# Local attention feeding a squared-ReLU MLP: attention output of tiles 6 and 7 transposed by DMA instead of on TensorE, with a new order of work

## The chip, the cores and the metric

The kernel runs on one core of a Trainium2 chip. The metric is the device time of one execution in microseconds (us); lower is better. The time before is 212.37 us, the median of five runs (211.97 to 212.8).

## The reference

Four batches, eight heads, 768 positions and head size 64. Each position sees eight global positions and the 96 positions up to itself, with a bias that grows with distance. The attention output, 3072 rows of 512, goes through two matrix products with a squared ReLU between them.

```python
scores = scale * np.matmul(q, k.transpose(0, 1, 3, 2))
is_global = pos[None, :] < int(n_global)               # n_global = 8
is_local = (rel >= 0) & (rel < int(n_local))           # n_local = 96
scores = scores + bias[None, :, :, :]
scores = np.where(is_global | is_local, scores, -1000000000.0)
a = np.exp(scores - np.max(scores, axis=-1, keepdims=True))
a = a / (np.sum(a, axis=-1, keepdims=True) + 1e-09)
x = np.matmul(a, v)              # then (B, S, H * D): 3072 x 512
h = x @ w_in                     # 512 -> 2048
g = np.maximum(h, 0.0) ** 2
return (g @ w_out).astype(np.float32)   # 2048 -> 512
```

## The kernel before

The 3072 rows are 24 tiles of 128 rows (index `j`, six per batch). Two tiles make a block of the MLP (index `blk`, 12 of them). A block's first product is done in eight steps `s1`, each 8 matmuls of 256 columns into one PSUM bank (L753); its second product is 16 steps `s2`, each 2 matmuls of 512 columns (L826).

For one tile the stages are:

- `load`: q, k and v are read by three DMAs on POOL's queue (L211). From tile 6 on, q and k go to a ring of three buffers, so that the load of tile j waits until the transposition of tile j-3 has read its buffer.
- `T`: q and k are transposed. Tiles 0 to 5 do it on TensorE (`tr`, L398) with a copy out of PSUM; from tile `JQK` = 6 on, one DMA transpose on SP's queue does it (L422). "T 12" below is this DMA for tile 12.
- `sc`: scores, 16 matmuls of 64 rows (8 for a batch's first tile) (L485). `exp` on ScalarE (L551), `mul` by the bias and mask on VectorE (L576).
- `pv`: probabilities times values, two halves of 8 matmuls (4 for a batch's first tile) (L638), and `norm` on VectorE, a reciprocal and a multiplication that write tile `x` (L665, L666).
- `xT`: `x` is transposed for the MLP. Tiles below `JX` do it with four TensorE transposes (`trx`, L701) and a copy out of PSUM by VectorE or ScalarE; tiles from `JX` on do it by one DMA transpose on SP's queue (L725). "xT 7" is this step for tile 7.

After `s1`, `relu` runs on ScalarE (L774) and the square `sq` on VectorE (L786). When a block's second product is complete, `o` copies it out of PSUM (L326 or L328) and `st` stores it by a DMA on SP's queue (L865); every block has two stores, "st 3" being those of block 3. At the end of the kernel the last block's second half is split in two.

So SP's queue carries the stores and all DMA transposes, in one order written at build time; what stands behind a DMA whose data is not ready waits with it.

The order of work on every engine is decided by `Plan.run` at build time, a list scheduler. Each operation has a cost, a set of predecessors and a `key`; the one with the earliest start (plus a small weight times its key) goes next. The tables `SHIFT` (by kind and tile), `LEADS` (by tile), `STEP` (after which `s1` step a tile's scores may come) and `HOLD` (which `s1` step waits for a tile's scores) move keys and predecessors. At run time the engines wait only for data and buffers; the order is fixed. Three one-element writes by VectorE (`gate`, L372) hold back the loads of tiles 8, 9 and 10; their predecessor in the plan is, among others, `xT_sp.get(j - 3)`, the DMA transposition of the output of tile j-3, where there is one.

The PSUM banks are a ring of six for everything but the sums of `s2`, which have two. `x` has two buffers: `norm` of tile j needs `x` of tile j-2 to have been transposed.

Of the kernel before, what the change touches and what calls it, by code (L numbers as in the profile page):

```python
# [21 lines left out]
class Plan:  # L22
# [8 lines left out]

    LAG = {"PE": 0.25, "ACT": 0.26, "DVE": 0.2, "SP": 0.6, "POOLQ": 0.8, "DMAQ": 1.2, "DMA": 0.0}
    URGE = 0.01
    SHIFT = {'T': -13, 'sc': -2.5, 'exp': -26, 'pv': -13, 'norm': -17, 'trx': -5, 'xT': 32, 'gk': -38, 'gv': -45, 'mul': -39, 'kl': 24, 's1': -3.5, 'relu': 8, 'sq': -13, 's2': -1.25, 'st': -30, ('mul', 4): 12, ('tr', 5): 18, ('T', 5): 8, ('norm', 5): -22, ('sc', 6): 16, ('pv', 6): 46, ('mul', 7): 29.5, ('gk', 7): -13, ('trx', 7): 12, ('sc', 8): -4, ('pv', 8): 9, ('norm', 9): -10, ('pv', 11): 14, ('pv', 12): 48, ('sc', 13): -14, ('pv', 14): 30, ('mul', 15): 17, ('norm', 17): 4, ('norm', 18): -36, ('exp', 19): -7, ('exp', 20): 14, ('pv', 20): 34, ('sc', 22): 10, ('s1', 2): -2.5, ('s1', 3): -32, ('sq', 3): 4, ('s1', 5): 9, ('s1', 6): 23.5, ('s1', 7): 34, ('s1', 8): -10, ('s2', 0): 7.5, ('s2', 2): -4, ('s2', 3): -27, ('s2', 4): 7.5, ('s2', 5): 22, ('s2', 6): 14, ('s2', 7): -4, ('s2', 8): -10, ('s2', 9): -8, ('s2', 10): -2}

    def shift(self, name):
        early = name[-1 if name[0] in ("T", "tr") else 1]
        return self.SHIFT.get(name[0], 0.0) + self.SHIFT.get((name[0], early), 0.0)

# [65 lines left out]
def kernel(  # L105
# [35 lines left out]
    NFIRST = 4  # L141
    NSPLIT = 4
    NBIAS = 3
    JQK, JX = 6, 8
    NQ, NKT = 3, 2 * TPB
    NG = 8 - NACC
    G = ("g", NG)
# [7 lines left out]
    def const(shape, dt, name):  # L155
        return consts.tile(shape, dt, name=name, tag=name)
# [18 lines left out]
    pbt = const([P, 2, P], FP32, "pbt")  # L175
    pbw = const([P, 2, P], FP32, "pbw")
    plan = Plan()
    LEADS = {5: 29.5, 6: 59, 7: 21, 8: 15, 9: 40, 10: 38, 11: 24, 12: 46, 13: 0, 14: 22, 15: 1, 16: -27, 17: 18, 18: -20, 19: 20, 20: 33, 22: 28, 23: 8}
    SAFE = {j: 1.6 for j in range(6, 12)} | {14: 4.2, 15: 3.2, 16: 3.5}
    SAFEX = {9: 1.5, 11: 1.5, 13: 2.5}  # L180

# [2 lines left out]
    JOIN = {(21, 0), (16, 0), (23, 0), (18, 0), (20, 0), (15, 0)}  # L184
    COPY = [14, 15, 19, 20, 22]
    BEHIND = {}
    HOLD = ((6, 0), (19, 0))
    STEP = {(17, 0): 58, (19, 0): 68, (4, 0): -7, (6, 0): 16, (11, 0): 24, (12, 0): 37}
    JGATE = 11
    NHS = 14  # L190
    NWARM = 8
# [68 lines left out]
    def emit_ones(e, js):  # L260
        for j in js:
            nc.vector.memset(v_sb[j][:, :, D : D + 1], 1.0)
# [38 lines left out]
    for g in range(NFIRST + 2, NT, 6):  # L301
        js = range(g, min(g + 6, NT))
        o = plan.op(
            ("ones", g), {"DVE": 0.2}, lambda e, js=js: emit_ones(e, js),
            key=-1.0, ready=15.0,
        )
# [40 lines left out]
    kl = [const([P, NPAIR, P], BF16, f"kl_{i}") for i in range(2 if COPY else 0)]  # L347
# [8 lines left out]
    for j in range(NT):  # L356
        b, t = divmod(j, TPB)
        first = t == 0
        need = 8 * (j // 2)
        base = need - LEADS.get(j, LEAD) + 4 * (j % 2)  # L360
        if (j, 0) in JOIN:
# [29 lines left out]
        for n in range(2) if j < JQK else ():  # L391
            users = []

            def emit_tr(e, j=j, n=n, fp=fp):
# [9 lines left out]
            tr = plan.op(  # L404
                ("tr", n, j), {"PE": 0.5 if fp else 0.24}, emit_tr,
                deps=[land["qk"[n], j]], key=base, takes=(*G, [users]),
            )
# [12 lines left out]
        if j >= JQK:  # L420
            def emit_dT(e, j=j, T_=T_):
# [5 lines left out]
            T = plan.op(  # L427
                ("T", j), {"SP": 1.3}, emit_dT,
                deps=[land["q", j], land["k", j], xT_op[j - 3]] + ku, key=base - 6,
            )  # L430
            T = plan.op(("moved", j), {"DMAQ": 1.2}, None, deps=[T])
            qk_users[slot(j)].append(T)
            if j in SAFE:

                T = plan.op(("seen", j), {"DMA": SAFE[j]}, None, deps=[T])
# [6 lines left out]
        mul, mul_users = {}, {}  # L442
# [55 lines left out]
        for gs in SETS.get(j, [tuple(range(groups))]):  # L498
            n = 8 * len(gs)
            sc_users = busers[2 * gs[0] : 2 * gs[-1] + 2]  # L500
            if (j, gs[0]) in JOIN:

                o, also, taken = joint
# [16 lines left out]
            if j < NBIAS:  # L520
# [6 lines left out]
            o = plan.op(  # L527
                ("sc", j, gs[0]), {"PE": 0.2 + 0.029 * n},
                lambda e, gs=also, f=emit_sc: f(e, gs), deps=[*deps, bias],
                key=base + 1 + 2 * gs[0], takes=takes,  # L530
            )
# [91 lines left out]
        norm = []  # L623
# [170 lines left out]
    for o in plan.ops:  # L794
        if o["name"][0] == "sc":
            j = o["name"][1]
            n = STEP.get(o["name"][1:], 4 * j - LEAD)
            if n >= 0 and j >= NFIRST:
                o["deps"].append(s1_ops[n // NSTEP, n % NSTEP])
                if o["name"][1:] in HOLD:  # L800
                    n += 1
                    s1_ops[n // NSTEP, n % NSTEP]["deps"].append(o)

    for blk in range(NBLK):
# [9 lines left out]
        for s, sub, half in order2:  # L814
# [5 lines left out]
            def emit_s2(e, blk=blk, s=s, sub=sub, half=half, w=w, cols=cols, own=own):  # L820
# [15 lines left out]
            o = plan.op(  # L836
                ("s2", blk, s, sub), {"PE": 0.43 * w / d_model}, emit_s2,
                deps=[d, land["wout", s]] + users[-1:],
                key=8 * blk + s + 2.0 + (0 if not last else 8 * sub + 8 * (half or 0)),
                takes=((*G, [users]) if own else ("acc", NACC, [users])) if s == 0 else None,  # L840
            )
# [6 lines left out]
            if s == NSTEP - 1:  # L848
# [14 lines left out]
                def emit_st(e, blk=blk, sub=sub, half=half, cols=cols):  # L863
# [7 lines left out]
                st = plan.op(  # L871
                    ("st", blk, sub), {"SP": 0.4}, emit_st,
                    deps=[ev, s1_ops[NLATE, 0] if blk < NLATE - 2 else None],
                    key=8 * blk + s + 9.0,
                )
                st = plan.op(("stored", blk, sub), {"DMAQ": 1.4}, None, deps=[st])
# [40 lines left out]
```

## Time and profile before

| | |
|---|---|
| Five runs | 211.97 to 212.8 us, median 212.37 |
| Profiled execution | 212.8 us, span from the first to the last instruction 211.0 |
| Granted TensorE clock | 1.00 |
| PE, VectorE, ScalarE, POOL busy | 204.0, 142.5, 119.4, 73.8 us |
| DMA queues, share of 16 engines' span | POOL's loads 88.0%, SP's stores and transposes 33.6% |

Times within the span are counted from its first instruction. A matmul's record is longer than the time until the next one can start, because matmuls overlap: the 768 matmuls of L753 have records of 273 ns each but follow each other every 109 ns or so (eight of them take 0.87 us in the chain of waits). Where a number of the prediction is a time on PE, it is taken from such stretches, not from the record of one matmul. About 24 of the 384 records of L826 are missing from this trace; the gaps that they leave are not waits.

### The profile page before, as it was taken

To read this page: it belongs to the slowest core of one execution; us is meant where nothing else is said; L and a number is where in the kernel's file an instruction comes from. 1 tells how busy PE (TensorE), PEld (TensorE's weight loads), DVE (VectorE), ACT (ScalarE), POOL (GpSimd) and SP (SyncE) were. 2 spreads that over 40 slices of the span, in tenths; PEclk is the share of its full clock that TensorE was granted. 3 is DMA by queue.
4 is the path that set the end of the run, shared out by engine and by line. 5 is a ranking of instruction groups with operands and counts; after the bars stand their busy time and mean duration, and the time that the engine had idled before them with its cause. 6 is when DMAs were issued, how large, how long until landed. Compare 5 with 4: busy or idle time off the path is not lost.

```text
span 211.0 us, 4998 instructions
## 1 busy us (share of the span) xinstructions
PE 204.0 (97%) x1960; PEld 142.9 (68%) x1984; DVE 142.5 (68%) x372; ACT 119.4 (57%) x222; POOL 73.8 (35%) x91
## 2 busy tenths in 40 slices
PE   7999999999999999999999999999999999999993
PEld 3777877666566856866856577686755766766862
DVE  7699688522887887883867684585785845953630
ACT  6787678134563754555753763754677436833531
POOL 8997675440638036422904040405400000000000
PEclk9999999999999999999999999999999999999999
DMA  9999999999799999999996979999933710310202
GB/s 131 146 174 187 183 191 199 175 161 235 77 173 130 211 114 126 201 169 137 149 175 71 198 83 96 144 131 134 141 105 75 169 33 3 124 26 3 99 0 99
DMA packets 112615, 27.32 MB, mean 129 GB/s; under 512 B 103248, under 2 KB 109648, under 8 KB 112592
## 3 DMA queue, kind: packets, MB, share of 16 engines
q0 software_dynamic: 79200, 13.37, 88.0%
q1 hardware_dynamic: 33392, 13.64, 33.6%
q8 instruction: 15, 0.25, 0.5%
q14 instruction: 8, 0.07, 0.1%
HBM read 27.26 MB, written 6.29 MB: 159 GB/s over the span
## 4 chain that ended last, share of the span: by engine, by line
PE 87%; DVE 7%; DMA 2%; issue 1%; ACT 1%
PE acc L826 38%; PE hT L753 36%; PE sc L485 5%; PE po L638 4%; DMA xT<-x 2%; DVE x L666 2%; PE warm L271 2%; PE tr L398 2%; DVE at L576 1%; DVE v L683 1%; DVE rs L665 1%; DVE qkT L328 1%; PE sc L465 1%; PE trx L701 1%; DVE hs L786 0%
## 5 line engine op out<-in xcount | busy, mean ns | idle before, releaser
L753 PE MATMUL hT<-xT,win 128*128 128x256 bf16 x768 | 94.2, 273 | 0.6 <-DMA xT<-x 0.4
L826 PE MATMUL acc<-wout,hs 128*128 128x512 bf16 (+1 forms) x376 | 90.1, 370 | 1.3 <-DVE rs L665 0.2
L774 ACT ACTIVATE hr<-hT 128x512 f32<-128x512 f32 x96 | 57.4, 605 | 54.7 <-PE hT L753 46.7
L753 PEld LDWEIGHTS <-win 128*128 128x128 bf16 x768 | 73.4, 98 | 17.9 <-issue 0.9
L786 DVE TENSOR_TENSOR hs<-hr 128x512 bf16<-128x512 f32 x96 | 65.3, 687 | 22.0 <-ACT hr L774 21.2
L826 PEld LDWEIGHTS <-hs 128*128 128x128 bf16 x400 | 36.9, 98 | 29.8
L551 ACT ACTIVATE esc<-sc 128x512 bf16<-128x512 f32 x78 | 40.4, 609 | 14.2 <-PE sc L485 13.4
L211 POOL DMA_DIRECT2D qk<-in_q_dram x23 | 20.6, 896 | 70.6 <-DMA qkT<-qk 52.7
L576 DVE TENSOR_TENSOR at<-esc,E 128x512 bf16<-128x512 bf16 x78 | 31.8, 421 | 8.7 <-ACT esc L551 6.3
L211 POOL DMA_DIRECT2D v<-in_v_dram x24 | 21.8, 910 | 1.4 <-DMA win<-in_moe_w_in_dram 1.0
L666 DVE TENSOR_TENSOR x<-po,rs 128x256 bf16<-128x256 f32 x48 | 20.4, 424 | 1.7
L211 POOL DMA_DIRECT2D qk<-in_k_dram x23 | 20.7, 906 | 0.5 <-DMA win<-in_moe_w_in_dram 0.5
L326 ACT COPY o<-acc 128x512 f32<-128x512 f32 (+1 forms) x20 | 11.2, 579 | 15.2 <-PE acc L826 15.1
L638 PEld LDWEIGHTS <-at 128*128 128x128 bf16 x352 | 15.8, 98 | 5.1 <-ACT at L551 0.5
L638 PE MATMUL po<-v,at 128*128 128x65 bf16 x352 | 17.6, 193 | 0.4 <-DVE v L683 0.2
L665 DVE RECIPROCAL rs<-po 128x4 f32<-128x4 f32 x48 | 8.5, 178 | 10.6 <-PE po L638 10.1
L485 PEld LDWEIGHTS <-qkT 64*128 64x128 bf16 x312 | 9.5, 94 | 6.1 <-issue 5.5
L485 PE MATMUL sc<-qkT 64*128 64x128 bf16 x192 | 12.9, 219 | 0.0
L485 PE MATMUL sc<-qkT,qkT 64*128 64x128 bf16 x120 | 8.6, 216 | 0.0
L328 DVE COPY o<-acc 128x512 f32<-128x512 f32 x5 | 3.5, 691 | 7.0 <-PE acc L826 7.0
L211 POOL DMA_DIRECT2D win<-in_moe_w_in_dram x8 | 6.2, 804 | 1.3 <-issue 0.5
L211 POOL DMA_DIRECT2D wout<-in_moe_w_out_dram x8 | 5.8, 720 | 2.1 <-DMA win<-in_moe_w_in_dram 2.0
(45 smaller groups left out, 69.1 us busy)
## 6 DMA issues: line engine op xcount, KB each, us to landing
out_dram<-o SPq DMA_DIRECT2D x23, 256.0 KB, 3.8
v<-in_v_dram POOLq DMA_DIRECT2D x24, 128.0 KB, 6.4
qk<-in_q_dram POOLq DMA_DIRECT2D x23, 128.0 KB, 4.7
qk<-in_k_dram POOLq DMA_DIRECT2D x23, 128.0 KB, 6.2
win<-in_moe_w_in_dram POOLq DMA_DIRECT2D x8, 256.0 KB, 8.0
wout<-in_moe_w_out_dram POOLq DMA_DIRECT2D x8, 256.0 KB, 9.1
qkT<-qk SPq DMA_TRANSPOSE x18, 5.5
plain<-in_q_dram SPq DMA_DIRECT2D x1, 256.0 KB, 3.3
```

The source lines that it names most:

```text
L211: nc.gpsimd.dma_start(out=dst, in_=src)
L326: nc.scalar.copy(dst, src)
L485: nc.tensor.matmul(out=tiles["sc", j, odd, g][:, at, :], lhsT=left[j - 1][half, pair, :] if kt else qkT[j % NKT][half, 1, pair, :], rhs=qk ...
L551: nc.scalar.activation(out=esc, in_=tiles.pop(("sc", j, odd, g)).rearrange("p a c -> p (a c)"), func=Act.Exp, scale=scale,)
L576: nc.vector.tensor_mul(at, tiles.pop(("esc", j, odd, g)), bias)
L638: nc.tensor.matmul(out=po[:, hi, :], lhsT=tiles["at", j, odd, g][:, at * P : (at + 1) * P], rhs=v_sb[kj][:, h, :], start=(i == 0), stop=(i ...
L665: nc.vector.reciprocal(rs, po[:, :, D : D + 1])
L666: nc.vector.tensor_tensor(out=x[:, 4 * hf : 4 * hf + 4, :], in0=po[:, :, :D], in1=rs.to_broadcast([P, 4, D]), op=Alu.mult,)
L753: nc.tensor.matmul(out=hT[:, c, :], lhsT=w_in_sb[s][:, kt, c * P : (c + 1) * P], rhs=tiles["xT", blk][:, kt, :], start=(kt == 0), stop=(kt ...
L774: nc.scalar.activation(hr, tiles.pop(("hT", blk, s)), Act.Relu)
L786: nc.vector.tensor_mul(hs, hr, hr)
L826: nc.tensor.matmul(out=tiles["acc", blk, sub, half], lhsT=hs[:, c, sub * P : (sub + 1) * P], rhs=w_out_sb[s][:, c, cols], start=(s == 0 an ...
```

## The change

`JX` goes from 8 to 6. The outputs of tiles 6 and 7, which are block 3 of the MLP, are transposed by two DMAs on SP's queue instead of by 8 TensorE transposes and two copies out of PSUM. The tables that steer the order are replaced by those that a search for an order found for this setting: `SHIFT` as a whole, `LEADS`, `HOLD` and `STEP`. What each engine computes is otherwise the same; the order of nearly all of it moves. POOL's order of loads stays as it was.

```diff
-    SHIFT = {'T': -13, 'sc': -2.5, ...
+    SHIFT = {'T': 8, 'sc': -22, ...
...
-    JQK, JX = 6, 8
+    JQK, JX = 6, 6
...
-    LEADS = {5: 29.5, 6: 59, 7: 21, 8: 15, 9: 40, 10: 38, 11: 24, 12: 46, 13: 0, 14: 22, 15: 1, 16: -27, 17: 18, 18: -20, 19: 20, 20: 33, 22: 28, 23: 8}
+    LEADS = {3: 28, 4: 6, 6: 74, 7: -2, 8: -5, 9: 38, 10: 38, 11: 16, 13: 33, 14: 18, 15: 68, 16: -108, 17: 26, 19: 8, 20: -18, 21: -26.5, 22: -16, 23: -9}
...
-    HOLD = ((6, 0), (19, 0))
-    STEP = {(17, 0): 58, (19, 0): 68, (4, 0): -7, (6, 0): 16, (11, 0): 24, (12, 0): 37}
+    HOLD = ((17, 0), (19, 0))
+    STEP = {(17, 0): 58, (19, 0): 70, (4, 0): -7, (11, 0): 25, (5, 0): -1, (9, 0): 28, (13, 0): 41, (23, 1): 81}
```

The built program's order on SP's queue, from the first transposition to tile 13, where "o" stands for one store:

```
before: o, T 6, T 7, o, o, T 8, o, T 9, xT 8, o, o, T 10, T 11, xT 9, T 12, o, o, xT 10, T 13
after:  T 6, o, o, T 7, o, o, xT 6, T 8, xT 7, T 9, xT 8, o, o, T 10, T 11, xT 9, o, o, T 12, xT 10, T 13
```

More of the change, by code (lines that the diff above doesn't have):

```diff
@@ L33 @@
     URGE = 0.01
-    SHIFT = {'T': -13, 'sc': -2.5, 'exp': -26, 'pv': -13, 'norm': -17, 'trx': -5, 'xT': 32, 'gk': -38, 'gv': -45, 'mul': -39, 'kl': 24, 's1': -3.5, 'relu': 8, 'sq': -13, 's2': -1.25, 'st': -30, ('mul', 4): 12, ('tr', 5): 18, ('T', 5): 8, ('norm', 5): -22, ('sc', 6): 16, ('pv', 6): 46, ('mul', 7): 29.5, ('gk', 7): -13, ('trx', 7): 12, ('sc', 8): -4, ('pv', 8): 9, ('norm', 9): -10, ('pv', 11): 14, ('pv', 12): 48, ('sc', 13): -14, ('pv', 14): 30, ('mul', 15): 17, ('norm', 17): 4, ('norm', 18): -36, ('exp', 19): -7, ('exp', 20): 14, ('pv', 20): 34, ('sc', 22): 10, ('s1', 2): -2.5, ('s1', 3): -32, ('sq', 3): 4, ('s1', 5): 9, ('s1', 6): 23.5, ('s1', 7): 34, ('s1', 8): -10, ('s2', 0): 7.5, ('s2', 2): -4, ('s2', 3): -27, ('s2', 4): 7.5, ('s2', 5): 22, ('s2', 6): 14, ('s2', 7): -4, ('s2', 8): -10, ('s2', 9): -8, ('s2', 10): -2}
+    SHIFT = {'T': 8, 'sc': -22, 'exp': 9.5, 'pv': -24, 'norm': -23.25, 'trx': -26.5, 'gk': -47.5, 'gv': -6.5, 'mul': 6.5, 'kl': -44.5, 's1': -1, 'relu': 78.5, 'sq': 28, 's2': 1, 'o': 50.5, 'st': -31, ('tr', 3): -8, ('sc', 3): 7, ('tr', 4): 1, ('mul', 4): -26, ('tr', 5): -2, ('T', 6): -59, ('sc', 6): 58, ('mul', 6): -28, ('pv', 6): 70, ('sc', 10): 28, ('pv', 10): 34, ('sc', 11): 38, ('pv', 11): 20, ('norm', 11): -13, ('norm', 14): 24, ('pv', 15): 65, ('pv', 16): -176, ('mul', 17): -17, ('norm', 18): 18, ('kl', 19): 84, ('norm', 19): 38, ('sc', 20): -17, ('pv', 20): -8, ('norm', 20): -7, ('mul', 21): 17, ('pv', 21): -2, ('sc', 22): 2, ('s1', 2): 2, ('s1', 3): -5, ('s1', 4): -6, ('s1', 5): -22, ('s1', 6): -12, ('sq', 6): -41, ('s1', 7): 14, ('sq', 7): -9, ('s1', 8): -8, ('s1', 10): 10, ('s1', 11): 25, ('s2', 0): 7.5, ('s2', 2): -4, ('s2', 7): 10, ('s2', 8): -12, ('s2', 9): 8, ('s2', 10): 10, ('s2', 11): 94}
     def shift(self, name):
```

## The prediction

> **What bounds the kernel now.** I read the page's busy times and clock first, then the list of waits of PE, then the chain of waits, and last the queue of SP and the landing times of its transposes.
>
> ```profile
> PE 204.0 (97%) x1960; PEld 142.9 (68%) x1984; DVE 142.5 (68%) x372; ACT 119.4 (57%) x222; POOL 73.8 (35%) x91
> PEclk9999999999999999999999999999999999999999
> ```
>
> PE is at work for the whole span at full clock, and no other engine is near it. A busy PE could still be waiting in small pieces, so the list of its waits comes next. Its largest entry after the start is this one (us in total, times, longest); the others are 0.2 or 0.3 us, in the start or at gaps that missing records leave:
>
> ```profile
> PE hT L753 <- DMA xT<-x: 0.4, 1, 0.4
> ```
>
> The chain shows the place, and with it what one stage costs on PE:
>
> ```profile
> 57.39 0.33 PE trx L701 x4
> ...
> 65.40 0.22 PE trx L701 x4
> ...
> 77.23 0.55 PE sc L485 x16
> ...
> 80.05 0.24 PE po L638 x8
> 80.29 0.86 PE acc L826 x4
> ...
> 86.22 0.87 PE hT L753 x8
> ...
> 139.71 4.92 DMA xT<-x
> 144.77 6.27 PE hT L753 x56
> ```
>
> So on PE an `s1` step is 0.87 us, an `s2` step (two matmuls) 0.43, the scores of a tile 0.55, a half of `pv` 0.24, the transposition of an output 0.22 (0.33 where it also pays for the switch out of the scores' 64 rows). After the start-up PE simply runs through its list; it can gain only what is taken off the list, the 0.4 us above, and part of the start, where the chain goes through VectorE for most of 9 to 20 us. It can lose wherever an input comes late. The inputs with the least certain times are the DMA transposes:
>
> ```profile
> 76.64 1.19 SPq L725 DMA_TRANSPOSE xT<-x  x1
> 77.93 1.50 SPq L422 DMA_TRANSPOSE qkT<-qk  x1
> 82.91 0.87 SPq L865 DMA_DIRECT2D out_dram<-o  x2
> 83.87 1.45 SPq L725 DMA_TRANSPOSE xT<-x  x1
> 85.43 1.32 SPq L422 DMA_TRANSPOSE qkT<-qk  x1
> ```
>
> The second row is T 12, issued at 77.93, ahead of the two stores of block 3 at 82.91. From issue to landing, T 12 and T 13 (the tile view of qkT from 76 to 92 us) took
>
> ```profile
> DMA to landing us min/median/max: 6.7/7.3/7.8
> ```
>
> The same view gives 7.9 and 9.1 us for T 10 and T 11 (66 to 74 us), but 3.0 for T 22 (156 to 163 us), when POOL's loads are over. The small output transposes `xT` took 3.6 and 5.5 us from 53 to 80 us and 2.4 from 180 us on. A transposition costs more than twice as much while loads are in flight, which is so until about 150 us.
>
> **Taken off PE.** Eight transposes with their weight loads: 0.33 + 0.22 = 0.55 us, of which 0.11 is the switch out of the scores, which the next group then pays. That leaves -0.45. The Trainium skill ("TensorE: Matmul & The Clock Gate", Part 4: PE-mode transpose) gives about 275 ns for a transpose within a kernel; eight would be 2.2 us, and the sum below would end near 211.5, a gain. The trace has four in 0.22 us, 55 ns each, pipelined, and the trace decides. The two copies out of PSUM (0.4 us each, on VectorE, which is busy 68%) are hidden behind PE and count nothing.
>
> **Start-up.** The order of the first 20 us changes. Up to the `norm` of tile 3, VectorE has two copies of transposed q/k less (0.43 each), one square less (0.69) and one output copy more (0.41): 1.1 us less. ScalarE has one copy more (0.6). PE's own waits there come to about 1.7 us, summed over the matmuls that start later than their kind's usual distance (from 5 to 20 us it is busy 14.4 us of 15 by the page's records, which overlap and so hide some of it). The bounds are -1.1, if VectorE's chain alone decides, and +0.6, if ScalarE's does; I take -0.2, since the first tiles still alternate between the two.
>
> **Added to SP's queue.** xT 6 and xT 7, each with an issue of 1.2 us. Everything else that is moved past them matters more. I take the order that was built for the changed kernel and add PE's prices between a result and its use. A tile's `x` is ready 0.95 us after its second `pv` has left PE (138.49 + 0.24 to 139.69), and SP comes to the next DMA 1.25 us after the end of a block's second `s2` sum where two stores stand before it (82.69 to 83.87 and a little more, since now both copies are ScalarE's).
>
> - T 8 now stands behind xT 6. From the second `pv` of tile 6 to the scores of tile 8 PE has 10 `s2`, 4 `s1`, one set of scores and two `pv`: 8.8 us. Less 0.95 and the 1.25 us of issuing xT 6, T 8 has 6.6 us. T 9, the nearest row with loads in flight, took 4.6. Hidden; 1.2 late at the worst of 7.8. T 8 lands about 5 us later than before, so POOL's loads of tiles 11 and 10 start later too; T 10 and T 11 have other things to wait for (below).
> - xT 7 to the first `s1` of block 3: 7 `s2`, 3 `s1`, scores, `pv`: 6.4, less 0.95, leaves 5.5 us against 3.6 to 5.5 measured. Hidden, just; 1.9 late if it took the 7.4 us of the slowest xT.
> - `x` has two buffers, so the `norm` of tiles 8 and 9 now waits for xT 6 and 7 to land. There are over 5 us to spare.
> - T 10 is behind the stores of block 2, as before. 9 `s2`, 4 `s1`, scores and two `pv` until its scores, 8.4 us; less 1.25 leaves 7.1 against 7.9 measured. Its queue held an xT and two stores just ahead then; xT 8 is now 4 us ahead. Between 0 and 2.0 (9.1 us); I take 0.3.
> - **T 12 is moved behind the stores of block 3.** They can't be issued before block 3 is complete, and SP holds T 12 until then. Behind T 12 are xT 10 and T 13, which still have 2 us or more, and POOL's load of tile 15, whose scores come some 20 us later. After that last `s2` PE has, until the scores of tile 12, scores 0.55, three `pv` 0.72, six `s1` 5.2 and two `s2` 0.86: 7.4 us. Less 1.25, T 12 has 6.1 us where it had over 11. By its own row (6.7) it is 0.6 late, by the median 1.2, by 9.1 it is 3.0; by the quiet 4.6 of T 9 it is not late. I take 1.2, for loads 13 and 14 should be in flight just then and the two stores stand ahead of it. PE serves its list in order, so all of it is lost. The skill's page "DMA: Bandwidth & Descriptors" (Latency and other measured facts; Anatomy of one DMA) has 261 GB/s for transposes and some 2 us fixed: 256 KB would take 3.0 us by that estimate, T 12 would be in time and the sum would be -0.65. T 22's 3.0 agrees, but only without loads; the 7.3 is from the stretch in question, and I go by it.
> - xT 15 to block 7: 12 `s2` and two short `pv` are 5.4 us, less 0.95, against a landing of 4.0: hidden. xT 17 to block 8: now 5.0 us of PE work instead of 5.46, which was 0.4 short; but the sums of block 6 are complete about 2 us of PE work earlier, so that the stores and T 19, which are ahead of xT 17, leave SP sooner. I leave the wait at 0.4, no change (0 to 0.9).
>
> **The sum.** -0.45 - 0.2 + 0.3 + 1.2 = +0.85. The profiled execution took 212.8 us with a span of 211.0, so 1.8 lie around the span; its span becomes 211.85 and its time 213.65. That execution was 0.43 above the median of the runs, so the median becomes 213.2.
>
> **Rivals.**
> First, nothing is late (faster): T 12 lands within 6.1 us of its issue. That is the point from which it decides. The 4.6 of T 9 speaks for it, and that the loads of tiles 13 and 14 start from the landings of T 10 and T 11, which could put them earlier than I think; 6.7 to 9.1 for its neighbours speak against. Then -0.45 - 0.2, and up to -0.4 more if block 8's wait goes: 211.3 to 211.7, say 211.5. Chance 0.25, of it 0.05 within 0.3%.
> Second, the transposes slow each other further: with 8.5 us each, T 10 is 1.4 late and T 12 2.4, so +3.15 and 215.5. The two more transposes and the late load of tile 11 speak for it; that the added work is some 2 us of a queue speaks against. Chance 0.12.
> Third, T 12 is late by about what is saved: 212.4. Chance 0.08.
> That the tables might leave the order as it was is excluded: the built order differs.
>
> **How the numbers follow.** 0.3% is 0.64 us, about what a measurement of this kernel can tell from no change. My forecast, T 12 late by 0.7 to 2.7, has 0.55, its own range is 212.7 to 214.7, and 0.08 of it is within 0.3%. Faster 0.20; same 0.05 + 0.08 + 0.08 = 0.21; slower 0.47 + 0.12 = 0.59. The range goes from the first rival's 211.4 to 215.4, just short of the second's centre.
>
> **What would show it.** Right: a wait of PE's scores (L485) for `DMA qkT<-qk` of 0.6 to 2.7 us near 89 us, with T 12 issued near 83 us straight after two stores; no `trx` after 45 us; PE's busy time down by 0.4 or so. Wrong: T 12 landing before 89 us; a wait of L753 for `DMA xT<-x` near 64 us of over half a us, which would make xT 7 the cause; a start of block 0 that has moved by more than half a us.

## The result and the profile after

The changed kernel takes 217.92 us in the median of ten runs (214.62 to 219.46), the kernel before, run beside it, 212.56 (211.97 to 213.22). Medians here and below count every run, while ratios leave out the runs that are more than 1.5% above the fastest of their kernel, so that the ratio here, 1.0137 [1.0106, 1.0167], rests on the five runs from 214.62 to 217.34 us, where the medians are 2.5% apart. The profiled execution, 219.44 us, is one of the longest. Where a cause rests on this one execution alone, the runs below test it.

First the page of the changed kernel: busy times, granted clock, the shares of the chain that ended last, and the group of the scores (busy, mean ns, then idle time before it and what ended it).

```profile
PE 204.6 (94%) x1951; PEld 142.1 (65%) x1976; DVE 140.4 (65%) x369; ACT 119.2 (55%) x223; POOL 73.9 (34%) x91
PEclk9999999999999999969999999999999999999999
PE 78%; DMA 12%; POOL 5%; issue 2%; ACT 1%; SPq 0%; POOLq 0%; ACTq 0%
L485 PE MATMUL sc<-qkT 64*128 64x128 bf16 x192 | 13.1, 222 | 4.8 <-DMA qkT<-qk 4.6
```

PE does about the same work (204.6 us of records, some of them at a lower clock), but its share of the span falls from 97% to 94%, one slice has a mean clock of 0.6, and DMA now has 12% of the chain, where it had 2%. The scores stood still for 4.8 us, 4.6 of them for transposed q and k. The list of PE's waits (us in total, times, longest) has the rest:

```profile
PE sc L485 <- DMA qkT<-qk: 4.6, 2, 2.8
PE hT L753 <- issue: 1.5, 1, 1.5
```

SP's queue, from the timeline, shows the place that the prediction named: T 12 (second row) straight behind the two stores of block 3.

```profile
83.99 0.82 SPq L865 DMA_DIRECT2D out_dram<-o  x2
84.91 2.92 SPq L422 DMA_TRANSPOSE qkT<-qk  x1
87.93 1.66 SPq L725 DMA_TRANSPOSE xT<-x  x1
89.69 1.25 SPq L422 DMA_TRANSPOSE qkT<-qk  x1
```

The chain of waits (start, length, what) shows both late transposes and what follows the second:

```profile
70.58 9.15 DMA qkT<-qk
79.73 0.05 issue
79.78 0.62 PE sc L485 x16
...
83.86 0.60 ACT o L326
84.46 0.02 issue
84.47 0.33 SPq L865
...
84.91 9.06 DMA qkT<-qk
93.97 0.05 issue
94.02 0.61 PE sc L485 x8
94.63 3.16 PE hT L753 x16
```

T 10 took 9.15 us, T 12 9.06. After T 12 the 16 matmuls of two `s1` steps took 3.16 us, where 2 x 0.87 = 1.74 is usual: 1.4 more. The scores just ahead of them took 0.61 us, 0.3 more than the same eight in the kernel before:

```profile
89.08 0.33 PE sc L485 x8
```

The windows (stretch, length, busy time and count of PE, PEld, DVE, ACT and POOL, granted clock, DMA share, GB/s) say why. The DMA share can pass 1, since the times of packets overlap.

```profile
90.00:94.00 4.00, 1.21 (x7) 0.50 (x6) 1.83 (x3) 1.20 (x2) 0.00 (x0) 0.98 1.72 145
94.00:98.00 4.00, 3.98 (x26) 2.79 (x27) 1.54 (x3) 2.66 (x5) 3.50 (x5) 0.59 0.94 102
98.00:102.00 4.00, 3.95 (x30) 2.23 (x29) 3.02 (x7) 0.60 (x1) 1.76 (x3) 1.00 2.18 139
```

PE is full from 94 to 98 us, but the clock granted is 0.59 in the mean. In steps of 1 us it is

```profile
93.00:94.00 1.00, 0.00 (x0) 0.00 (x0) 0.00 (x0) 0.00 (x0) 0.00 (x0) 0.93 0.78 155
94.00:95.00 1.00, 0.98 (x11) 0.67 (x12) 0.00 (x0) 0.34 (x1) 0.50 (x1) 0.50 1.09 239
95.00:96.00 1.00, 1.00 (x6) 0.72 (x5) 0.65 (x2) 1.00 (x3) 1.00 (x2) 0.50 0.00 0
96.00:97.00 1.00, 1.00 (x7) 0.72 (x5) 0.90 (x2) 0.72 (x2) 1.00 (x2) 0.50 1.26 81
97.00:98.00 1.00, 1.00 (x8) 0.68 (x7) 0.00 (x0) 0.60 (x1) 1.00 (x3) 0.87 1.39 89
```

so it was 0.50 for about 3.4 us, and half of that, 1.7, is what the scores and `s1` lost (0.3 + 1.4). PE stood still just before, for 2.8 us.

The wait put down to "issue" is in block 7. Here the chain has

```profile
135.84 0.59 ACT o L326
136.43 1.30 issue
137.73 3.65 PE hT L753 x32
```

and names no releaser, but xT 15 was issued at 131.27 and landed at 137.64, 0.09 us before PE goes on; it took 6.4 us against 4.0 before.

The profiled executions are 6.64 us apart (219.44 and 212.8). Two waits for q and k 4.6, low clock 1.7, block 7 1.5, less the wait of 0.4 in block 8 that this execution of the changed kernel doesn't have, less the 0.45 forecast for the transposes: 6.95, which leaves 0.3 unexplained.

### The profile page after: what moved, and what is told of

Its sections match the earlier page's. It is cut to its first block, busy times and chain, and to the rows that moved or that the text cites. A ratio compares the mean times of both kernels' runs of the same rounds, so it can differ in the third digit from the quotient of the medians.

```text
span 217.7 us, 4968 instructions
## 1 busy us (share of the span) xinstructions
PE 204.6 (94%) x1951; PEld 142.1 (65%) x1976; DVE 140.4 (65%) x369; ACT 119.2 (55%) x223; POOL 73.9 (34%) x91
## 3 DMA queue, kind: packets, MB, share of 16 engines
HBM read 27.26 MB, written 6.29 MB: 154 GB/s over the span
## 4 chain that ended last, share of the span: by engine, by line
PE 78%; DMA 12%; POOL 5%; issue 2%; ACT 1%; SPq 0%; POOLq 0%; ACTq 0%
PE acc L826 35%; PE hT L753 34%; DMA qkT<-qk 8%; PE sc L485 4%; PE po L638 4%; DMA win<-in_moe_w_in_dram 3%; POOL qk L211 2%; POOL v L211 2%; ACT o L326 1%; POOL win L211 1%; PE tr L398 0%; SPq L865 0%; PE trx L701 0%; POOL pbi L265 0%; SPq L422 0%
## 5 line engine op out<-in xcount | busy, mean ns | idle before, releaser
L753 PE MATMUL hT<-xT,win 128*128 128x256 bf16 x768 | 93.2, 275 | 2.3 <-issue 1.5
L826 PE MATMUL acc<-wout,hs 128*128 128x512 bf16 (+1 forms) x375 | 88.2, 370 | 1.3
L753 PEld LDWEIGHTS <-win 128*128 128x128 bf16 x768 | 73.9, 99 | 16.8 <-issue 2.3
L774 ACT ACTIVATE hr<-hT 128x512 f32<-128x512 f32 x96 | 56.6, 604 | 46.7 <-PE hT L753 29.9
L786 DVE TENSOR_TENSOR hs<-hr 128x512 bf16<-128x512 f32 x96 | 64.1, 686 | 15.9 <-ACT hr L774 14.9
L551 ACT ACTIVATE esc<-sc 128x512 bf16<-128x512 f32 x78 | 40.6, 611 | 28.4 <-PE sc L485 26.8
L485 PE MATMUL sc<-qkT 64*128 64x128 bf16 x192 | 13.1, 222 | 4.8 <-DMA qkT<-qk 4.6
L485 PEld LDWEIGHTS <-qkT 64*128 64x128 bf16 x312 | 9.5, 95 | 12.0 <-DMA qkT<-qk 5.6
L638 PE MATMUL po<-v,at 128*128 128x65 bf16 x352 | 17.1, 193 | 0.1
L485 PE MATMUL sc<-qkT,qkT 64*128 64x128 bf16 x120 | 8.6, 216 | 0.0
L612 DVE COPY qkT<-qkT 128x32 bf16<-128x32 bf16 x11 | 2.0, 183 | 7.0 <-PE sc L485 6.9
```

The costliest lines, as they stand in the source:

```text
L485: nc.tensor.matmul(out=tiles["sc", j, odd, g][:, at, :], lhsT=left[j - 1][half, pair, :] if kt else qkT[j % NKT][half, 1, pair, :], rhs=qk ...
L551: nc.scalar.activation(out=esc, in_=tiles.pop(("sc", j, odd, g)).rearrange("p a c -> p (a c)"), func=Act.Exp, scale=scale,)
L638: nc.tensor.matmul(out=po[:, hi, :], lhsT=tiles["at", j, odd, g][:, at * P : (at + 1) * P], rhs=v_sb[kj][:, h, :], start=(i == 0), stop=(i ...
L753: nc.tensor.matmul(out=hT[:, c, :], lhsT=w_in_sb[s][:, kt, c * P : (c + 1) * P], rhs=tiles["xT", blk][:, kt, :], start=(kt == 0), stop=(kt ...
L774: nc.scalar.activation(hr, tiles.pop(("hT", blk, s)), Act.Relu)
L786: nc.vector.tensor_mul(hs, hr, hr)
```

## The experiments

All ratios are to the kernel before, run on the same chip beside each kernel. Orders were changed by moving one operation in the finished list, without planning anew:

```python
done = plan.run(...)
def place(name, where, other):
    o = next(o for o in done if o["name"] == name and o["emit"])
    done.remove(o)
    at = max(i for i, x in enumerate(done) if x["name"] == other)
    done.insert(at + (where == "after"), o)
```

| kernel | what differs | median us | ratio [95%] |
|---|---|---|---|
| after_again | changed kernel | 218.32 | 1.0272 [1.0206, 1.0338] |
| before_dma67 | before, DMA transposes of tiles 6 and 7 | 212.95 | 1.0013 [0.9974, 1.0051] |
| before_t12_late | before, T 12 behind st 3 | 212.96 | 1.0039 [1.0005, 1.0073] |
| jx6_alone | before, only `JX = 6` | 215.04 | 1.0124 [1.0082, 1.0167] |
| tensor_again | changed, tiles 6 and 7 on TensorE | 214.46 | 1.0120 [1.0052, 1.0189] |
| t12_first | changed, T 12 ahead of st 3 | 213.78 | 1.0077 [1.0038, 1.0116] |
| t8_first | changed, T 8 ahead of xT 6 | 217.13 | 1.0213 [1.0150, 1.0276] |
| t8_t12_first | both moves | 214.19 | 1.0077 [1.0050, 1.0105] |
| t10_t12_first | T 10 ahead of st 2, T 12 ahead of st 3 | 214.34 | 1.0062 [1.0011, 1.0113] |
| v_early | changed, three loads of v earlier | 214.78 | 1.0011 [0.9945, 1.0078] |
| v_early_again | the same, more runs | 213.58 | 1.0038 [1.0016, 1.0060] |
| v_t12 | v_early and t12_first | 214.35 | 1.0070 [1.0034, 1.0106] |
| before_v | before, the same three loads earlier | 212.22 | 0.9996 [0.9979, 1.0013] |
| v_early2 | v_early, three more loads of v earlier | 213.14 | 1.0012 [0.9990, 1.0035] |
| fill12 | changed, ten unused matmuls ahead of T 12's scores | 216.13 | 1.0210 [1.0145, 1.0275] |

**The changed kernel once more (after_again).**

> The changed kernel once more, unchanged, for a second profile. In the first one PE waited 1.9 us for the transposed q/k of tile 10, 2.6 us for tile 12 and 1.7 us for the output of tile 15, and right after the 2.6 us the granted clock was 0.59 for 4 us. Queue theory (T 10 and T 12 behind stores on SP's queue): both waits are there again, of 0.5 to 3 us each, whatever the total. Clock theory (a wait that is long enough brings the clock down, and that is what makes some executions some 3 us longer than others): where the wait for tile 12 is below 2 us the clock stays at 1.00 and the time is near 215; where it is over 2.5 us the clock falls and the time is 217 to 219.5.

The wait for T 12 is there again, with its row in PE's waits and the clock (slices of 5.4 us):

```profile
PE sc L485 <- DMA qkT<-qk: 2.9, 1, 2.9
PEclk9999999999999999958999999999999999999999
```

T 12 took 9.2 us (83.11 to 92.36). In steps of 1 us the clock shows 0.50 for about 6.8 us here. T 10 took 7.0 and was in time, so its wait of 1.8 in the first profile varies from execution to execution; that of T 12 is in both.

**The parts of the change, one at a time.** The DMA transposes of tiles 6 and 7 in the order of before:

```diff
-    (trx and its copy out of PSUM)             # for j >= 6
+    nc.sync.dma_start_transpose(out=xT of j, in_=x of j)
+    place(('xT', 6), 'after', ('norm', 6, 1))
+    place(('xT', 7), 'after', ('norm', 7, 1))
```

> One part of the change alone: the kernel before, in its own order of work, with the outputs of tiles 6 and 7 transposed by DMA, each issued on SP as soon as its x is ready (in the built order xT 6 stands behind T 8, xT 7 ahead of T 9; everything else stands as it did). Order theory (the DMAs as such are hidden; the new order is what costs): xT 7 lands near 65.5 us where block 3 wants it at 66.5, PE has 0.45 us less to do, 211.8 to 212.8 us, T 12 still lands before 86. DMA theory (two more transposes in the crowded stretch from 55 to 70 us set off late inputs, here as in the run with JX alone, which lost 2.8 us): waits of 1 us or more at block 3, tile 10 or tile 12, and 213.5 to 215.

No difference from before that can be told (the interval reaches from 0.3% faster to 0.5% slower, so a gain of 0.45 us would not show), with the 0.4 us in block 8 as the one wait for an `xT` in its profile. The transposes themselves are hidden. The place of T 12 alone, in the order of before:

```diff
+    place(('T', 12), 'after', ('st', 3, 1))
```

> The kernel before with one DMA moved: the transposition of q/k of tile 12 is issued behind the two stores of block 3, as in the changed kernel, and nothing else. Queue theory: T 12 is issued near 84 us instead of 78 and lands near 91 to 93, where the scores of tile 12 want it at 89: a wait of 1 to 3 us for it, time 213.5 to 215.5, more where the clock falls after it. Load theory: no wait of over 0.5 us, 212.2 to 213.

0.4% slower, and in its profile no wait of the scores at all; its largest wait in total, 1.5 us, is for weights near the start. The view of qkT from 76 to 95 us has T 13 and T 12:

```profile
DMA to landing us min/median/max: 3.2/3.9/4.5
```

T 12 behind the same two stores took 4.5 us here, not 9. So neither part alone makes T 12 late. The changed order with tiles 6 and 7 back on TensorE:

```diff
+    if j < 8:
+        (four transposes into trx, tensor_copy out of PSUM)
+        return
```

> The changed kernel's order of work as it is, but the outputs of tiles 6 and 7 are transposed on TensorE again (8 transposes and two copies by VectorE, at the places where the two DMAs were issued). Queue theory: the stores still stand ahead of T 10 and T 12, so the waits for tiles 10 and 12 stay (1 to 3 us each), plus 0.45 us for the transposes: 215 to 219. Load theory: without the two DMAs T 8 and the loads of tiles 11, 10 and 12 are early again, the waits go, and the time is 212.5 to 213.5.

T 12 stands behind the stores there and takes 6.0 us (83.71 to 89.66): just in time, no wait of the scores. After the start its profile, of an execution of 213.63 us, has one wait over 0.3 us (the edit moves L753 to L762):

```profile
PE hT L762 <- ACT o L326: 0.7, 1, 0.7
```

Still the kernel is 1.2% slower than before [0.5 to 1.9], so the new order (here with both copies on VectorE) costs something without the two DMAs as well. Of its four runs two took 215.29 and 216.09 us; where those lost time no profile shows. And `JX = 6` alone, with the planner free to order the rest by the old tables:

```diff
-    JQK, JX = 6, 8
+    JQK, JX = 6, 6
```

> The kernel before with JX set to 6 and its own tables kept, so that the planner orders the two DMA transposes with the old keys. In the built order T 8 stays ahead of xT 6, T 12 stays ahead of the stores of block 3, and xT 6 to 8 follow each other. DMA theory (the two DMAs themselves cost, whatever the order): 214 or more. Order theory (the loss is in where the search put the queue's entries): 211.5 to 213.5, if the planner's new order has no late input of its own.

The planner put T 12 behind the stores of block 3 here as well (stores from 82.24, T 12 at 83.35), against what the expectation assumed. T 12 took 9.4 us, and the profile has

```profile
PE sc L485 <- DMA qkT<-qk: 1.8, 1, 1.8
PE hT L753 <- DMA xT<-x: 1.0, 1, 1.0
```

So in these profiles a late T 12 comes of the two together, T 12 behind the stores and the DMA transposes of tiles 6 and 7 ahead of it, under either set of tables.

**T 12 back to its place (t12_first).**

```diff
+    place(('T', 12), 'before', ('st', 3, 0))
```

> The changed kernel with one DMA moved: the transposition of q/k of tile 12 is issued on SP's queue ahead of the two stores of block 3, as in the kernel before, and nothing else. Queue theory: the wait for tile 12 (2.6 us) is gone and with it the fall of the clock after it (1.4 us); the wait for tile 10 stays at 0.5 to 2 us; time 213.0 to 214.5, and all runs close together. Load theory (the two added output transposes and the later loads that follow from them fill the DMA queues from 55 to 95 us, so tile 12 is late wherever it stands): still a wait of over 1 us for tile 12 and a time of 215 or more.

About 4.5 us of the 6 come back. T 12 took 4.0 us (78.16 to 82.16), and no score waits for it. What is left stands elsewhere:

```profile
PE hT L753 <- DMA xT<-x: 2.5, 2, 1.5
```

These are block 5 (T 13 now takes 9.9 us, beside load 15, and xT 11 lands behind it) and block 8 (xT 17, 5.7 us).

**Is it the delay of T 8 that is handed on?** T 8 starts 3.5 us later than before, behind xT 6, and the loads of tiles 11 and 12 with it.

```diff
+    place(('T', 8), 'before', ('xT', 6))
```

> The changed kernel with one DMA moved: the transposition of q/k of tile 8 is issued ahead of the transposition of the output of tile 6, so that it no longer waits for that output. T 12 stays behind the stores of block 3. Train theory (new, from the runs so far: xT 6 ahead of T 8 makes T 8 land at 59.5 instead of 55 to 56, so the loads of tiles 11, 10, 12 and at last 14 come 2 to 3 us later, and load 14 then runs beside T 12, which takes 9 us instead of 4.5 to 6): T 8 lands near 56, load 14 starts near 79.5, T 12 takes 5 to 6.5 us, the wait for tile 12 falls from 2.6 to 3.0 us to under 1, and the time is 213 to 215. Queue theory alone (its place behind the stores is what makes T 12 late): the wait stays at 2 us or more, 216 to 219.

It is not undone so. The wait for T 12 is still there, and xT 7, now behind a longer queue, comes 1.5 us late to block 3:

```profile
PE sc L485 <- DMA qkT<-qk: 2.6, 1, 2.6
PE hT L753 <- DMA xT<-x: 1.5, 1, 1.5
PEclk9999999999999999979999999999999999999999
```

That theory fell in this form: load 14 was issued at 82.67, between the 81.17 and 83.18 of the changed kernel's two profiles. Adding the move of T 12, or one of T 10, gives nothing beyond t12_first:

> Both moves together: T 8 ahead of xT 6 and T 12 ahead of the stores of block 3. If place and train are the two parts of the loss, neither tile 10 nor tile 12 waits for more than 0.5 us and the time is 212 to 213.5, near the kernel before. If there is a third part of more than 1 us (waits at blocks 5, 7 or 8 for xT 11, 15 or 17, which the run with T 12 moved showed with 1.2 and 1.7 us), it stays at 213.5 or more.

> The changed kernel with T 10 ahead of the stores of block 2 and T 12 ahead of the stores of block 3, nothing else. The run with T 12 alone moved gave 213.8. Queue theory: T 10 and T 11 land 1 to 2 us earlier, the wait for tile 10 is gone where there was one, and the loads of tiles 13 and 14 come earlier: 213.0 to 213.8. If T 10's wait for its own load (k of tile 10 lands near 69 to 69.5 us) sets its issue, moving it changes nothing: 213.5 to 214.3.

**What T 12 shares the DMA engines with.** The same transposition behind the same two stores took from 4.5 to 9.4 us. Set side by side by the three DMAs of the load of tile 14, in us from the span's start (v stands apart, since it is issued last):

| kernel | q of load 14 issued, k landed | v issued, landed | T 12 issued, landed | T 12 took |
|---|---|---|---|---|
| before_t12_late | 79.17, 84.27 | 80.91, 85.16 | 84.70, 89.23 | 4.5 |
| tensor_again | 79.51, 84.86 | 81.25, 85.71 | 83.71, 89.66 | 6.0 |
| v_early (below) | 80.46, 86.36 | 49.28, 57.29 | 83.36, 89.49 | 6.1 |
| fill12 (below) | 80.54, 87.20 | 82.28, 90.36 | 82.91, 90.96 | 8.1 |
| after_again | 81.17, 89.06 | 82.91, 92.27 | 83.11, 92.36 | 9.2 |
| jx6_alone | 81.56, 89.95 | 83.30, 92.74 | 83.35, 92.76 | 9.4 |
| t8_first | 82.67, 89.86 | 84.40, 94.07 | 85.34, 94.28 | 8.9 |
| changed, first profile | 83.18, 91.00 | 84.92, 94.10 | 84.91, 93.97 | 9.1 |

In the last five rows v of load 14 is issued less than 1 us from T 12, lands within 0.6 us of it, and is about as slow as T 12 itself (8.1 to 9.7 us). Where it was issued 2.5 us or more ahead, in the first two rows, it took about half as long. Below are this v's issue and its time to landing in the changed kernel's first profile, and its time to landing in tensor_again:

```profile
84.92 0.92 POOL L211 DMA_DIRECT2D v<-in_v_dram  x1
DMA to landing us min/median/max: 9.2/9.2/9.2
DMA to landing us min/median/max: 4.5/4.5/4.5
```

So the slow T 12 and load 14 are in flight together and both are slow; T 22, with no load beside it, takes 3.0 in all. To test whether that load is the cause, it was made smaller while SP's order stayed as it was: the loads of v for tiles 12 to 14, which need no ring buffer, come straight behind the load of tile 8. The edit adds six lines, so that L753 is L759 in these kernels.

```diff
-                load_tile(j)
+                load_part(0, j)
+                load_part(1, j)
+                if j not in (12, 13, 14):
+                    load_v(j)
+                if j == 8:
+                    for x in (12, 13, 14):
+                        load_v(x)
```

> The changed kernel with the loads of v of tiles 12, 13 and 14 issued right behind the load of tile 8, when POOL stands idle, instead of with their tiles' q and k; v has a buffer per tile, so nothing waits for it. That takes a third of the load traffic out of the stretch in which T 10, T 11 and T 12 go (from 67 to 90 us). Contention theory (T 12 takes 9 us because it shares the DMA engines with load 14): T 12 takes 6.5 to 8 us, its wait falls to 0.3 to 1.5 us, time 215 to 217 instead of 218; the loads moved ahead may delay T 7 and T 8 by 1 us. Queue theory alone (what counts is only its late issue near 84 us): the wait for T 12 stays at 2.5 us or more, 217.5 to 219.5.

> The kernel with the v loads of tiles 12 to 14 behind the load of tile 8 and nothing else different from the changed kernel, with more rounds. Theory: contention between T 12 and load 14 is the larger part of what was lost, so T 12 takes 6 to 7 us from issue to landing where it took 9.1 to 9.2, and the median is 213 to 215. Rival (the short time of its first profile was chance): the median is over 216 and the profile shows a wait of scores for qkT of over 2 us.

This fits the theory, with an effect larger than expected; v of tiles 12 and 13 moved too, so the test is of these loads together. In the first profile T 12 is still behind the stores (second row of SP's timeline), and the view of qkT has it as the larger of two:

```profile
82.44 0.82 SPq L871 DMA_DIRECT2D out_dram<-o  x2
83.36 2.00 SPq L428 DMA_TRANSPOSE qkT<-qk  x1
...
DMA to landing us min/median/max: 3.7/4.9/6.1
```

It landed 6.1 us after its issue, no score waited, and that execution took 211.89 us, less than the kernel before in the median. Two of the four runs, 215.6 and 216.0, have a clock of 0.992, as the longer runs of the changed kernel do, so a long wait may have come there; no profile has caught it. In the longer series one run of 22 has that clock, the median is 213.58, T 12 took 5.9 in the profile, and there is one wait that counts, 2.1 us for xT 17 in block 8:

```profile
PE hT L759 <- DMA xT<-x: 2.1, 1, 2.1
```

Do the two remedies add, and does the earlier load gain anything where T 12 is in time?

> The changed kernel with both edits that gave something singly: the v loads of tiles 12 to 14 come behind the load of tile 8, and T 12 stands ahead of the stores of block 3. Theory (T 12's place costs only because load 14 is beside it, and the standing still brings the clock down): either edit alone already takes away the wait for T 12, so both together give hardly more than the better of them: 212.5 to 214, with no wait of scores for qkT. Rival (place and contention are two separate costs that add): 211.5 or below.

> The kernel before with the v loads of tiles 12 to 14 behind the load of tile 8. Theory: the order of before has no wait that these loads decide, so nothing is to be had: 212.2 to 212.8, within 0.3% of before. Rival (the stretch of 60 to 95 us is short of bandwidth in any order): 0.5 us or more faster. If it should be slower, the moved loads are in the way of loads 9 to 11.

Neither. Both remedies together give no more than one of them, which fits that they act on the same wait; the profile of v_t12 can't confirm it, for it is of an execution of 741.16 us, far from all others. In the kernel before, the earlier loads change nothing. What they gave in the changed kernel is put down to T 12 for that reason, and because the wait for it is gone from both profiles. The last wait was tried in the same way:

```diff
-                if j not in (12, 13, 14):
+                if j not in (12, 13, 14, 20, 21, 22):
...
-                if j == 8:
-                    for x in (12, 13, 14):
+                if j in (8, 16):
+                    for x in range(j + 4, j + 7):
```

> The kernel with the v loads of tiles 12 to 14 behind the load of tile 8, and besides the v loads of tiles 20 to 22 behind the load of tile 16. The longer runs of the first edit had a wait of 2.1 us for xT 17 at block 8, with load 22 beside it. Theory (what is left of the loss is the same contention at loads 20 to 22): the wait for xT 17 goes, the median falls by about 1 us to 212 to 212.8, and some runs are below 211.5, where the changed kernel would be the faster one. Rival (xT 17 is late for its place behind T 18, xT 16 and T 19 in the queue, or for something else): the median stays at 213.2 to 213.9 with the wait of 1 to 2 us in block 8.

xT 17 still took 5.9 us and PE waited for it, against the theory, so the v of load 22 was not what held it:

```profile
PE hT L759 <- DMA xT<-x: 1.6, 1, 1.6
```

The median is 0.4 us lower than that of v_early_again, but their intervals overlap (one of its 22 runs took 539.16 us and counts in the median). This is the best of the variants, and it is level with the kernel before (1.0012, within what can be told apart); none of those tried beats it.

**The clock.** Ten matmuls of 512 columns on zeros, about 2.2 us of work whose result nobody reads, are put ahead of the scores of tile 12, so that PE does not stand still.

```diff
+    FILL = {12: 10}
...
+            if j in FILL:
+                fill = ps_g.tile([P, 4 * P], FP32, name="fill", tag="g")
+                for i in range(FILL[j]):
+                    nc.tensor.matmul(out=fill, lhsT=zero[:, :P], rhs=zero, start=True, stop=True)
```

> The changed kernel with ten matmuls of 512 columns on zeros (2.2 us) added on PE just ahead of the scores of tile 12, into a bank of their own, their result unused. They fill the wait for T 12, so that PE stands still for 0.3 to 0.8 us instead of 2.6 to 2.9. Clock theory (standing still for over 2 us is what brings the granted clock to 0.59 for some 4 us): the clock stays at 1.00 and the time falls by 1 to 1.6 us, to 216.5 to 217.5, although work was added. Otherwise (the clock falls for another reason, a load on the chip or the mean rate of work): the clock falls as before and the time is the same or up to 0.5 us longer, 218 to 219.5.

Although 2.2 us of work was added, the median is 2.2 us below that of after_again, and the clock is 1.00 in all four runs (0.984, 0.991, 0.992 and 1.00 in those of after_again). The intervals overlap, and T 12 also happened to land 1.2 us sooner after its issue, so the size of the clock's part rests on the 1.7 us counted in the profile. That is 0.8% of the span, so a clock of 0.992 is what one such stretch leaves, 0.984 two. In the ten runs of the result the six from 217.34 us up have 0.984 to 0.992, the four near 215 have 0.998 or more.

The clock is not all of the spread, though: the longest run of after_again, 219.33 us, and that of fill12, 218.34, are both listed with 1.00. And 1.00 is listed, too, where an execution left no record of the clock, as in the profile of v_early_again, whose page has no row for it.

## Why the prediction was wrong in size and right in kind

- **Direction and place: right.** T 12 issued straight after two stores near 84 us, a wait of L485 for `DMA qkT<-qk`: both came as described, the wait just above the 0.6 to 2.7 us named. xT 7 was in time (landed at 63.97, no wait in block 3), as costed, and xT 6 and 7 by themselves cost nothing that can be told (before_dma67).
- **T 12's landing: the step that failed, a term that was mis-sized.** The prediction gave T 12 6.1 us before it is late, and that holds: 5.9, 6.0 and 6.1 were in time. It then took the median of 7.3 for the landing, and with it 1.2 us; the landing was 9.1 and 9.2, the wait 2.8 and 2.9, which is the upper end that it had written down (3.0). The 7.3 came from T 12 and T 13 of before. But T 12 had load 13 beside it there and no store just ahead (the stores of block 3 come 5 us later), and load 14 came behind it (79.71 against 77.93). In its new place it has two stores just ahead and the v of a load at its side. The fitting row was T 10 of before, behind the two stores of block 2 and issued 0.2 us after the v of load 12, which landed 0.2 us after it:

```profile
66.71 0.93 SPq L865 DMA_DIRECT2D out_dram<-o  x2
68.18 0.90 POOL L211 DMA_DIRECT2D v<-in_v_dram  x1
68.35 5.09 SPq L422 DMA_TRANSPOSE qkT<-qk  x2
DMA to landing us min/median/max: 7.9/8.5/9.1
```

The last line is that of T 10 and T 11. The prediction had these rows, 7.9 and 9.1, and used them for T 10 and as a bound only.

- **Load 14's time: not in the working.** The prediction saw that T 8 and the loads behind it start later, and dropped it since "T 10 and T 11 have other things to wait for". But the loads of tiles 13 and 14 wait for T 10 and T 11 to have read their buffers. Load 14 is issued at 81.17 and 83.18 instead of 79.71, and so its v goes out together with T 12. Where it is issued earlier, at 79.17 in before_t12_late, T 12 is not late in the same place. What makes load 14 late is argued only: it is issued at 79.51 with TensorE transposes in the same order, but also at 79.30 in before_dma67, which has the two DMAs in the order of before, and the move of T 8 alone did not undo it.
- **The clock: missing from the sum.** The prediction counted a wait as the time that PE stands still. This one also cost 1.7 us afterwards.
- **T 10: 0.3 taken, with bounds of 0 and 2.0;** 1.8 in one profile and 0 in the next. In the first it took 9.15 us, beside the v of load 12 again.
- **xT 15 and block 7: taken as hidden, 1.5 us late.** The working used the landing of before, 4.0; beside load 20 it was 6.4. t10_t12_first has a wait of 1.6 us there too.
- **xT 17 and block 8: unchanged 0.4, bounds 0 and 0.9.** It is 0 in the first profile of the changed kernel, where everything before is late, but 2.1 and 1.6 in v_early_again and v_early2. In the profile of v_early xT 17 took 2.5 us, nothing was late after the start, and the time was 211.89: the first rival (nothing late, 211.5) as described. Only single runs come near it, the lowest at 211.24.
- **Start-up: -0.2 taken.** Block 0 starts at 15.27 and 15.61 us in the two profiles of the changed kernel, at 15.70 before: less than the half us that it had set as a sign of being wrong.
- **Transposes taken off PE: -0.45.** The last `trx` starts at 40.6 us, as forecast none after 45, but no run shows the 0.45 by itself; PE's busy time rose, by the lower clock.

The second rival (transposes slowed to 8.5 us each, 215.5) was nearest: it has T 12 and T 10 late by 2.4 and 1.4. It stopped short of the measured 217.92 by the clock and by block 7. That the right wait came at the right place follows from the working; that the upper figure of 3.0 for it was nearly met is in part luck, for it took the slowest of four rows, T 11's, and gave no reason for T 12 to be like it.

What stays open: why T 12 and the load beside it take 8 to 9.7 us when issued together, and what part the two stores have in it; what delays load 14; what the new order costs in tensor_again; and what makes xT 17 take 5.7 to 6.4 us in three of the variants (2.5 in the profiles of v_early and t10_t12_first), against 4.9 in the kernel before.

## What to carry to other kernels

Cost a moved DMA by a row that had the same company at its issue, not by the row of the same DMA in its old place: ask which loads will be in flight when it starts, and what sets their start. Two delays that are hidden or cheap alone, here a queue position and two more transposes, can meet in one transfer, so follow the change through buffer releases to the next loads before calling it hidden. Where a wait can come near the 2.6 to 2.9 us that brought the clock down here, add the cost of a lower clock after it.

## What was not expected of the hardware

- The clock fell to 0.50 after PE had stood still for 2.6 (t8_first), 2.8 and 2.9 us, for about 3.4 us in the first two and 6.8 in the third. It stayed at 1.00 after the 1.8 us for T 10. After 2.1 us (v_early_again) the pace shows no fall: the next 56 matmuls took 6.29 us, against the 6.27 of the same 56 before. The Trainium skill ("TensorE: Matmul & The Clock Gate", Why this matters for your kernels) warns of gaps above about 3 us; here somewhat less was enough.

```profile
146.66 6.29 PE hT L759 x56
```

- The same DMA transposition of 256 KB took 3.0 us with no load in flight and up to 10.6 beside one (T 19 of the kernel before; 9.9 for T 13 in t12_first). Its issue on SP takes longer too, 2.92 us for T 12 where 1.25 is usual.
- A few us in the time of issue went with a factor of two: in t12_first T 12 was issued 1.4 us ahead of load 13 and landed in 4.0 us; in the changed kernel it was issued 1.7 us behind the q of load 14, together with its v, and both took 9 us. Whether the order of issue or the amount in flight decides, these runs don't separate.
